# Diagonal-block inversions moved from GpSimd to VectorE, and a range check moved from VectorE to GpSimd, in a DeltaNet + PReLU kernel

## Chip, cores, metric

One core of one Trainium2 chip. The metric is the device time of one execution in microseconds (us), as the median of the runs of one kernel. All runs quoted here were in the fast state. The aim is to predict, from the profile of the kernel before alone, what the change does to the time, and then to find out by experiments which part of it did what.

## The reference

```python
def _attn_ref(q, k, v, beta):            # B=4, H=8, S=768, D=48
    k_n = k / (np.linalg.norm(k, axis=-1, keepdims=True) + 1e-06)
    state = np.zeros((B, H, D, D), dtype=np.float32)
    for t in range(S):
        kt, vt, bt = (k_n[:, :, t], v[:, :, t], beta[:, :, t, None])
        y[:, :, t] = np.einsum('bhd,bhde->bhe', q[:, :, t], state)
        v_old = np.einsum('bhde,bhd->bhe', state, kt)
        state = state + bt[:, :, :, None] * np.einsum('bhd,bhe->bhde', kt, vt - v_old)

def _moe_ref(x, w_in, w_out, alpha):     # x: 3072 x 384 (from y), w_in: 384 x 2048, w_out: 2048 x 384
    h = x @ w_in
    g = np.maximum(h, 0.0) + alpha * np.minimum(h, 0.0)
    return g @ w_out
```

The weights `w_in` and `w_out` arrive as float64 and are converted to fp32 on the chip.

## The kernel before

The attention runs in 24 steps (12 chunks of 64 tokens, two pairs of batches). Each step needs the inverse of triangular 64 x 64 matrices, which is built from inverses of their 32 x 32 diagonal blocks. These are computed by elimination in seven batches: the first on VectorE, the other six on GpSimd. In parallel the weights are converted in 56 pieces (24 of `w_in` with 256 columns, 32 of `w_out` with 192), each of which passes ScalarE (two instructions), VectorE (two), GpSimd (an add) and VectorE again (the range check, which sets numbers too small for fp32 to zero). `weave` mixes the instruction streams, and each engine runs its own in order.

Names used below: `inv` is the inverse of a step's matrix, built from the diagonal blocks (`diag`), the masked key products `kk` and an intermediate `mid`; `r` is the step's right-hand side, `u` its scaled product with `inv`, and `a_t` the masked products of queries and keys. The FFN is the part with `w_in` and `w_out`, and `g` is its hidden layer after the activation. "u of step 0 reaches TensorE" is the start of the first matmul that reads it.

```python
# one piece of the weights' conversion; temp(...) has two buffers
last = temp("last")
nc.scalar.activation(last, lo, ACT.Copy, scale=2.0**-29)
size = temp("size").bitcast(FP32)
nc.scalar.square(size, hi.bitcast(FP32))
high = dst.bitcast(U32)
nc.vector.tensor_scalar(out=high, in0=hi, ...)              # L179
nc.vector.scalar_tensor_tensor(out=high, in0=hi, ...)       # L183
nc.gpsimd.tensor_tensor(out=high, in0=high, in1=last, op=ALU.add)          # L187
nc.vector.scalar_tensor_tensor(out=dst, in0=size, scalar=LEAST * LEAST, in1=dst,
                               op0=ALU.is_ge, op1=ALU.mult)                # L188
# ... (cut)
def eliminate(m, eng):                   # batch m; HB = 32
    r = block[m][0:np_]
    for j in range(1, HB - 1):
        # ... prod = 0:np_ partitions x j*(31-j)
        eng.tensor_tensor(out=prod, in0=..., in1=..., op=ALU.mult)                    # L362
        eng.tensor_tensor(out=r[:, 0:j, j + 1 : HB], in0=r[:, 0:j, j + 1 : HB],
                          in1=prod, op=ALU.add)                                       # L368
        yield
    nc.gpsimd.memset(r.rearrange("p r c -> p (r c)")[:, :: HB + 1], 1.0)              # L372
    flipped = work.tile([128, HB, HB], FP32, name="flipped", bufs=1)
    eng.tensor_copy(out=flipped[0:np_], in_=r.rearrange("p r c -> p c r"))            # L374
    # ... (two DMAs to DRAM, from which each step fetches its blocks)
# ... (cut)
FIRST = [b[0] for b in batches]          # batch 1 is woven into step 0, batch 2 into step 4, ...
for n in range(N):
    gens = [(attention(n), 4)]
    if n + 2 in FIRST:
        gens.append((eliminate(place[n + 2][0], nc.gpsimd), HB - 1))
    # ... 5 pieces of w_in in each of steps 0 to 3; from step 4 on FFN and w_out
    weave(*gens)
```

## Time and profile before

| | before |
|---|---|
| time, median of 3 runs | 887.39 us (887.05 to 888.3) |
| TensorE busy | 748.6 us |
| u of step 0 reaches TensorE (L472) | 97.6 us |
| conversion of `w_out`, first VectorE instruction to last check | 176.3 to 260.5 us |
| first matmul of the FFN's second product (L530) | 259.2 us |

The profile's first page of the kernel before: span, busy time of each engine (PE is TensorE, PEld its weight loads, DVE VectorE, ACT ScalarE, POOL GpSimd), and for three engines the busy share in 40 equal slices of 22.1 us, in tenths.

```profile
span 885.7 us, 20961 instructions
PE 748.6 (85%) x8917; PEld 574.9 (65%) x8917; DVE 289.2 (33%) x731; ACT 181.2 (20%) x402; POOL 281.6 (32%) x507
PE   4310678813779999999999999999999999999998
DVE  4870545514761313323233132131221312213030
POOL 5158522387330005811007700028447300000000
```

From the 13th slice on TensorE is full. What is to be gained lies in the slices before, where its digits fall to 0 and 1 while GpSimd (POOL) shows 8.

### The profile page before, as it was taken

Reading aid. Unit: us, or ns where it says so; the run is one execution under the profiler, and the core shown is the slowest. Engines: PE = TensorE matmul, PEld = TensorE weight load, DVE = VectorE, ACT = ScalarE, POOL = GpSimd, SP = SyncE. Lnnn points to the kernel's source line nnn. Section 1 sums busy time; section 2 is a strip of 40 time slices with the busy share of each in tenths; the row PEclk is TensorE's granted clock in tenths of the full one; section 3 lists DMA queues with packets and bytes.
Section 4 is the critical chain, followed back from the end, with each engine's and each line's share of the span. In section 5 each row is a group of like instructions: output and inputs, shape, how many; then the busy total and the mean of one; then the engine's idle time right before and its main releaser. Section 6 shows DMA issues by size and latency. Waiting matters only on the chain.

```text
span 885.7 us, 20961 instructions
## 1 busy us (share of the span) xinstructions
PE 748.6 (85%) x8917; PEld 574.9 (65%) x8917; DVE 289.2 (33%) x731; ACT 181.2 (20%) x402; POOL 281.6 (32%) x507
## 2 busy tenths in 40 slices
PE   4310678813779999999999999999999999999998
PEld 3210667712556868768778687786877868778684
DVE  4870545514761313323233132131221312213030
ACT  2210233312341202213112121120211212112020
POOL 5158522387330005811007700028447300000000
PEclk9999978555789999999999999999999999999999
DMA  5771166621353323062221252311422311000000
GB/s 102 158 158 42 26 174 159 143 78 47 99 144 63 61 42 64 23 117 58 56 56 33 57 111 39 69 38 28 105 48 42 73 31 22 1 20 2 10 10 18
DMA packets 183549, 58.10 MB, mean 66 GB/s; under 512 B 168592, under 2 KB 175776, under 8 KB 183456
## 3 DMA queue, kind: packets, MB, share of 16 engines
q1 hardware_dynamic: 183008, 56.66, 29.1%
q8 instruction: 70, 1.15, 0.5%
q10 hardware_dynamic: 448, 0.11, 0.1%
q14 instruction: 23, 0.19, 0.1%
HBM read 39.43 MB, written 17.30 MB: 64 GB/s over the span
## 4 chain that ended last, share of the span: by engine, by line
PE 77%; POOL 8%; DVE 7%; issue 3%; DMA 3%; SPq 1%; ACT 1%; POOLq 0%; ACTq 0%; DVEq 0%
PE p_ffn L530 28%; PE p_ffn L510 28%; POOL block L368 4%; POOL prod L362 3%; PE p_one L472 3%; PE p_one L415 3%; PE p_big L443 3%; PE p_one L458 3%; PE p_big L303 2%; PE p_one L404 2%; PE p_big L276 2%; PE p_one L499 1%; PE p_big L478 1%; DVE prod L362 1%; DVE block L368 1%
## 5 line engine op out<-in xcount | busy, mean ns | idle before, releaser
L510 PE MATMUL p_ffn<-xt,w_in 128*128 128x256 f32 x1152 | 274.4, 394 | 22.2 <-DVE g L521 19.8
L510 PEld LDWEIGHTS p_ffn<-xt,w_in 128*128 128x128 f32 x1152 | 222.1, 197 | 57.2 <-DVE g L521 14.1
L530 PE MATMUL p_ffn<-w_out,g 128*128 128x384 f32 x768 | 257.6, 489 | 0.0
L530 PEld LDWEIGHTS p_ffn<-w_out,g 128*128 128x128 f32 x768 | 143.1, 190 | 91.4
L521 DVE SCALAR_TENSOR_TENSOR g<-low,al_t,p_ffn 128x256 f32<-128x256 f32 x192 | 84.0, 477 | 178.9 <-ACT low L518 178.9
L362 POOL TENSOR_TENSOR prod<-block 128x30 f32<-128x30 f32 (+19 forms) x180 | 87.5, 486 | 41.1 <-DMA block<-image 22.9
L368 POOL TENSOR_TENSOR block<-block,prod 128x30 f32<-128x30 f32 (+19 forms) x180 | 92.9, 516 | 13.3
L518 ACT ACTIVATE low<-p_ffn 128x512 f32<-128x512 f32 x96 | 57.3, 596 | 167.9 <-PE p_ffn L510 159.1
L428 POOL TENSOR_TENSOR v_raw<-v_raw,norm 128x384 f32<-128x384 f32 x24 | 19.9, 830 | 211.0 <-DMA v_raw<-in_v_dram 204.2
L266 POOL TENSOR_TENSOR mask<-minus,wgt 128x512 f32<-128x512 f32 x24 | 25.2, 1049 | 104.5 <-DVE kk L309 86.4
L404 PE MATMUL p_one<-diag,kk 64*64 64x32 f32 x768 | 30.6, 231 | 25.3 <-POOL prod L362 21.5
L458 PE MATMUL p_one<-r,inv 64*64 64x48 f32 x768 | 31.6, 239 | 23.8 <-POOL prod L362 23.8
L415 PE MATMUL p_one<-diag,mid 64*64 64x32 f32 x768 | 30.9, 235 | 23.4 <-ACT mid L407 22.8
L458 PEld LDWEIGHTS p_one<-r,inv 64*64 64x64 f32 x768 | 28.5, 154 | 33.4 <-POOL block L368 23.9
L415 PEld LDWEIGHTS p_one<-diag,mid 64*64 64x64 f32 x768 | 28.3, 152 | 31.4 <-ACT mid L407 23.3
L404 PEld LDWEIGHTS p_one<-diag,kk 64*64 64x64 f32 x768 | 28.5, 149 | 27.1 <-POOL prod L362 21.6
L472 PEld LDWEIGHTS p_one<-u,a_t 64*64 64x64 f32 x768 | 27.4, 149 | 20.4 <-DVE u L460 9.4
L472 PE MATMUL p_one<-u,a_t 64*64 64x48 f32 x768 | 30.5, 234 | 11.6 <-DVE u L460 11.6
L174 ACT ACTIVATE last<-words 128x192 uint32<-128x192 uint32 (+1 forms) x56 | 22.5, 401 | 87.0 <-POOL w_in L187 45.0
L537 ACT COPY o_sb<-p_ffn 128x384 f32<-128x384 f32 x24 | 11.5, 479 | 129.4 <-PE p_ffn L530 129.4
L446 DVE TENSOR_TENSOR r<-v_raw,p_big 128x384 f32<-128x384 f32 x22 | 12.2, 553 | 69.9 <-PE p_big L443 68.6
L486 DVE TENSOR_TENSOR y<-y,p_one 128x384 f32<-128x384 f32 x22 | 12.2, 554 | 59.6 <-PE p_one L472 59.6
(75 smaller groups left out, 619.4 us busy)
## 6 DMA issues: line engine op xcount, KB each, us to landing
image<-kk SPq DMA_DIRECT2D x24, 256.0 KB
words<-in_moe_w_in_dram SPq DMA_DIRECT2D x24, 256.0 KB
words<-in_moe_w_out_dram SPq DMA_DIRECT2D x32, 192.0 KB
ke<-in_k_dram SPq DMA_DIRECT2D x48, 96.0 KB
qp<-in_q_dram SPq DMA_DIRECT2D x48, 96.0 KB
v_raw<-in_v_dram SPq DMA_DIRECT2D x48, 96.0 KB
kl<-in_k_dram SPq DMA_DIRECT2D x48, 96.0 KB
out_dram<-o_sb SPq DMA_DIRECT2D x48, 96.0 KB
```

What stands on the lines that cost most here:

```text
L266: nc.gpsimd.tensor_tensor(out=mask, in0=minus[:, None, :].to_broadcast([128, H, C]), in1=wgt.rearrange("p a g -> p (a g)")[:, :, None].to_ ...
L362: eng.tensor_tensor(out=prod, in0=r[:, 0:j, j : j + 1].to_broadcast([np_, j, n]), in1=r[:, j : j + 1, j + 1 : HB].to_broadcast([np_, j, n] ...
L368: eng.tensor_tensor(out=r[:, 0:j, j + 1 : HB], in0=r[:, 0:j, j + 1 : HB], in1=prod, op=ALU.add)
L404: nc.tensor.matmul(p[half(t), h], kk[n][half(t), h], diag[n % NE][half(t), h, 0:HB])
L415: nc.tensor.matmul(p[half(t), h], mid[n % 2][half(t), h], diag[n % NE][half(t), h, HB:C])
L443: nc.tensor.matmul(p[half(t), a, w, g], x[n][dims(a), g, half(t)], state[bp][dims(a), t, g])
L458: nc.tensor.matmul(p[half(t), h], inv[n % NE][half(t), h], rhs_[n][half(t), h])
L472: nc.tensor.matmul(p[half(t), a, g], a_t[n][half(t), a * G + g], us[n][half(t), a * G + g])
L510: nc.tensor.matmul(p_h[:, i], w_in[:, t, (f + i) * 128 : (f + i + 1) * 128], xt[:, t], start=(t == 0), stop=(t == KT - 1),)
L518: nc.scalar.activation(low, p_h, ACT.Relu, scale=-1.0)
L521: nc.vector.scalar_tensor_tensor(out=g[:, i], in0=low[:, i], scalar=al_t[:, f + i : f + i + 1], in1=p_h[:, i], op0=ALU.mult, op1=ALU.add,)
L530: nc.tensor.matmul(p_o, gs[f // 2][:, f % 2, bp * 128 : (bp + 1) * 128], w_out[:, f], start=(f == 0), stop=(f == FT - 1),)
```

## The change

The intent: take the inversions, which TensorE waits for, from the slower engine to the faster one (an elimination instruction of 128 x 238 elements takes 0.62 us on GpSimd in the kernel before and 0.40 on VectorE in the kernel after), and make room for them on VectorE by giving GpSimd the range check and small products.

```diff
             nc.scalar.square(size, hi.bitcast(FP32))
+            nc.gpsimd.tensor_scalar(
+                out=size, in0=size, scalar1=LEAST * LEAST, scalar2=None, op0=ALU.is_ge
+            )
@@
             nc.gpsimd.tensor_tensor(out=high, in0=high, in1=last, op=ALU.add)
-            nc.vector.scalar_tensor_tensor(
-                out=dst, in0=size, scalar=LEAST * LEAST, in1=dst,
-                op0=ALU.is_ge, op1=ALU.mult,
-            )
+            nc.gpsimd.tensor_tensor(out=dst, in0=dst, in1=size, op=ALU.mult)
@@ prep: two products of 128 x 8 per step
-        bt = beta_t[:, c, bp]
-        nc.vector.tensor_tensor(out=bt, in0=bt, in1=rec, op=ALU.mult)
-        nc.vector.tensor_tensor(
+        nc.gpsimd.tensor_tensor(out=beta_t[:, c, bp], in0=beta_t[:, c, bp], in1=rec, op=ALU.mult)
+        nc.gpsimd.tensor_tensor(
             out=wgt,
@@ through_state: no copy for the first chunk (the two steps with c == 0); solve() indexes accordingly
+        if c == 0:
+            rhs_[n] = by_parity(nv[n])
+            return
         r = work.tile([128, H, D], FP32, name="r")
-        if c == 0:
-            nc.gpsimd.tensor_copy(out=r.rearrange("p (a g) d -> p a g d", a=2), in_=by_parity(nv[n]))
-            rhs_[n] = r
-            return
@@ the loop over steps
         if n + 2 in FIRST:
-            gens.append((eliminate(place[n + 2][0], nc.gpsimd), HB - 1))
+            gens.append((eliminate(place[n + 2][0], nc.vector), HB - 1))
```

In the kernel after, the lines are L178 (compare), L190 (add), L191 (multiply), L361 and L367 (elimination), L458 (u), L470, L508 and L528 (matmuls that were L472, L510 and L530).

> **What bounds the kernel now.** I first cut the span into five stretches, with the busy time of each engine in each (after the engines: granted TensorE clock, DMA share, GB/s).
>
> ```profile
> 0.00:53.00 53.00, 19.00 (x273) 14.57 (x273) 35.77 (x109) 12.32 (x29) 17.32 (x40) 1.00 0.67 127
> 53.00:104.00 51.00, 12.49 (x264) 12.08 (x265) 14.56 (x41) 8.04 (x23) 37.95 (x70) 1.00 0.27 68
> 104.00:176.00 72.00, 58.04 (x1193) 51.18 (x1191) 40.98 (x104) 24.21 (x61) 21.07 (x29) 0.74 0.63 149
> 176.00:260.00 84.00, 38.46 (x377) 30.94 (x376) 44.96 (x123) 28.07 (x79) 52.78 (x94) 0.65 0.36 100
> 260.00:886.00 626.00, 620.58 (x6819) 466.16 (x6817) 152.97 (x357) 108.53 (x211) 152.45 (x276) 1.00 0.22 46
> ```
>
> From 260 us on TensorE is busy 620.6 of 626 us at full clock. That part is a fixed amount of matmul: it starts when the weights' conversion and attention steps 0 to 5 are done, and the end follows 626 us later. So the change gains only by an earlier start of that part, and loses wherever VectorE makes TensorE wait inside it. Before it TensorE is idle in two blocks, both while GpSimd (POOL) inverts a batch of diagonal blocks. The timelines of TensorE, VectorE and GpSimd there:
>
> ```profile
> 57.31 0.23 POOL L362 TENSOR_TENSOR prod<-block 128x30 f32<-128x30 f32 x1
> 86.85 0.71 DVE L188 SCALAR_TENSOR_TENSOR w_in<-size,w_in 128x256 f32<-128x256 f32 x1 [23.49 <-POOL w_in L187]
> 93.53 1.91 POOL L374 COPY flipped<-block 128x1024 f32<-128x1024 f32 x1
> 97.61 1.83 PE L472 MATMUL p_one<-u,a_t 64*64 64x48 f32 x29 [7.14 <-DVE u L460]
> ```
>
> The inversion runs on GpSimd from 57.3 to 95.4 us. One add of the weights' conversion (L187) stands behind most of it in GpSimd's order, VectorE's range check (L188) waits 23.5 us for that add, and u of step 0, behind the check, reaches TensorE at 97.6. The second block is the same from 174.9 to 213.6 us, with two such waits (17.7 and 10.2 us). The chain that ended last agrees: 77% of it is TensorE, 8% GpSimd, 7% VectorE.
>
> **What the skill says, and the trace.** "SBUF — State Buffer", section "Who interferes with whom": a VectorE instruction with two SBUF inputs, or in a two-port mode, and a GpSimd instruction that reads SBUF exclude each other; the later one blocks. The trace agrees, at a point where v_raw ran on GpSimd from 49.00 to 49.83 and a copy from 49.90 to 50.40:
>
> ```profile
> 48.88 0.24 DVE L362 TENSOR_TENSOR prod<-block 64x84 f32<-64x84 f32 x1
> 49.15 0.77 DVE L368 TENSOR_TENSOR block<-block,prod 64x84 f32<-64x84 f32 x1
> 49.96 0.51 DVE L362 TENSOR_TENSOR prod<-block 64x58 f32<-64x58 f32 x1
> 50.50 0.21 DVE L368 TENSOR_TENSOR block<-block,prod 64x58 f32<-64x58 f32 x1
> ```
>
> The same size takes 0.24 us free and 0.77 us blocked. Likewise L183 on 192 elements: 0.35 free, 0.75 blocked (medians of 14 each). Instructions reading PSUM (g at L521, u at L460) keep 0.47 and 0.55 us either way.
> "VectorE: DVE Perf Modes", section on the TRN2 errata, gives (N+151)/0.96 ns for an fp32 tensor_tensor: 407 ns at N = 240; the trace has 400. "GPSIMD Engine Reference", section 3.1, has 2.6 cycles per element for two inputs on GpSimd and about 1.8 for a tight loop; the trace's mask (512: 1.05 us) and v_raw (384: 0.83 us) give 0.17 us + 1.7 ns per element, less than 2.6 cycles at the page's 1.2 GHz (2.2 ns) would be.
>
> **Part by part.**
> *Inversion on VectorE.* A batch has 60 tensor_tensor on j(31-j) elements, 4960 summed over j, so 9920 in all. On VectorE (batch 0, rows by shape: 30 elements 0.19 us, 240 elements 0.40) one costs 0.16 us + 1 ns per element: 60 x 0.16 + 9.9 = 19.5, plus 60 gaps of 0.035 = 21.6 us, plus 1.0 for the flip. On GpSimd it took 38 us with what stood between. Six batches move: two (45 us) before the matmul-bound part, four (90 us) inside it.
> *Range check to GpSimd.* VectorE loses 56 instructions (32 of 0.34, 24 of 0.41: 21 us) and with them every wait for the add. GpSimd gets a compare and a multiply per piece. Estimates from its other rows: compare like a copy (384: 0.51 us) 0.40 us for 192 elements and 0.46 for 256; multiply by the fit above 0.50 and 0.61. With the add (0.60, 0.74) and three gaps of 0.08 a piece is 1.75 us (w_out) or 2.05 us (w_in), against 0.6 and 0.74 before. GpSimd becomes the pace of the conversion: 32 x 1.75 = 56 us for w_out.
> *Weights' small products (beta_t, wgt) to GpSimd and no copy of the right-hand side.* 48 small instructions of 0.2 us move to where there is room, two copies of 0.5 us go; none on the path. About 1 us.
>
> *Stretch 53 to 104.* I read the compiled instruction orders of the two kernels against each other: TensorE's is practically the same; on VectorE u of step 0 comes after 48 of the 60 inversion instructions and four conversion pieces. Inversion starts near 59.6 (a_t, three pieces, three norms ahead of it), 48 instructions are 18.2 us, the conversion between 3.2, blocking by GpSimd perhaps 2: u at 83 instead of 97, a gain of 14 us. The inverse goes out later in the DMA queue, behind kk of step 6, which shifts by the same 14.
> *Stretch 104 to 176.* Bursts of three to five conversion pieces now pass at 2.05 us on GpSimd instead of 1.3 to 1.7, and ScalarE's copies stand behind them (two buffers for its temporaries). One to two us in each of three steps: a loss of 3. Net 11 us earlier at the end of the stretch, r of step 5 near 165.
> *Stretch 176 to 260.* From r of step 5 to the end of the conversion it took 84 us. After: 13 inversion steps first (10 us), then GpSimd has 96 instructions of mean 0.50 us and 0.08 gap, and VectorE about 99 that exclude it. Each then blocks the other; the trace shows GpSimd's instructions little lengthened (0.59 to 0.64) and VectorE's doubled (0.35 to 0.75), so I take 0.58 + 0.10 per GpSimd instruction: 65 us, with mask, v_raw and the flip 70. Sum 80 to 81, a gain of 3 us. I chose this over full serialization (below). So the matmul-bound part starts 14 us earlier.
> *Inside the matmul-bound part.* An attention step is 31.5 us there (start to start of L443). VectorE's own work is 7.7 us of it (153/626); an inversion adds 22.6, and some blocking: over 30 us, so VectorE is full for that step. Walking the new VectorE order of step 8: inversion starts at 350.6, and g for the second-last L510 group is done near 370.8 instead of 365.9. TensorE starts L530 at 366.7 and its third p_ffn tile needs that buffer (two of them): about 4 us of waiting. In steps 12, 16 and 20 fewer g lie in the inversion, but inv and a_t come late: 1, 1 and 1 to 2 us. Sum 7 to 8.
> The sum: 887.4 - 14 + 7 = 880.
>
> **Rivals.** (1) *The lock makes the conversion as slow as before.* If in the stretch from 176 every VectorE and GpSimd instruction simply added up, it would be 10 + 96 x 0.86 = 93 us instead of 84, the 11 us gained earlier would shrink to 2, and with 7 lost later the time would be about 892; for it speaks that GpSimd and VectorE together are already busy 98 of 84 us there. Against it: their overheads overlap. (2) *VectorE becomes the bound in the steps with an inversion.* If TensorE waits 6 to 8 us in each of four, the loss is 24 to 32 us: about 900. For it: over 30 of 31.5 us; against: an inversion needs to be ready only for the step after next, and the static order leaves 4 to 7 us of FFN matmuls between each product and its use. (3) *The long waits vanish altogether.* TensorE idles 38 us from 53 to 104 and 45 us from 176 to 260; if the conversion flows freely beside the inversion on VectorE and the chain follows TensorE, 30 to 35 us are gained and nothing is lost later: about 855. For it: no instruction on the attention path now waits for GpSimd's in-order queue behind an inversion.
>
> **Range and chances.** Mid 880. The front may gain from 2 (rival 1) to 30 us (rival 3), the later part may lose 2 to 25 us; they are independent, so 8 in 10 is 860 to 898. Over 2% faster is below 869.6, over 2% slower above 905. Faster 0.25 (mostly rival 3), same 0.68, slower 0.07 (rival 2 together with rival 1).
>
> **What would show it.** Right: in the profile after, u of step 0 reaches L472 near 83 us; conversion's multiply on GpSimd ends near 246; GpSimd busy about 1.5 us per piece; VectorE busy about 289 - 21 - 9 + 6 x 20.5 (inversions without gaps) = 382 us, plus 20 or more of blocking; TensorE busy unbroken from about 246 us except for waits on g, r or a_t from VectorE in four steps, 7 us together. Wrong: inversion instructions on VectorE well over 0.6 us on average in the front (the lock rules: rival 1); waits of TensorE for g over 5 us in several later steps (rival 2); L530 of the first chunk starting before 235 us (rival 3). The estimate that carries most is GpSimd's compare and multiply: at 0.8 us each the conversion alone takes 76 us and the gain is gone.

## The result, and the profile after

| | before | after |
|---|---|---|
| time, median (range) of 4 runs each | 887.22 us (886.69 to 888.3) | 873.2 us (872.68 to 874.94) |
| ratio, 95% interval | | 0.9844 (0.9827 to 0.9861) |
| mean granted TensorE clock of the profiled run | 0.945 | 0.950 |

The ratio here and below is the mean time of one kernel's fast runs over that of the kernel before's fast runs of the same rounds, so it is not quite the ratio of the medians. The change gains 14 us or 1.6%: the interval of the ratio lies clear of 1. But it is within 2%, so it counts as "same". The output is correct.

The first page of the kernel after, the same rows, with the chain that ended last:

```profile
span 870.9 us, 20922 instructions
PE 745.9 (86%) x8917; PEld 571.9 (66%) x8917; DVE 389.9 (45%) x993; ACT 182.9 (21%) x402; POOL 185.1 (21%) x299
PE   4311886463499999999999999999999999999998
DVE  3789736786513227724037632248439403213030
POOL 6242758588740010001001001000000000000000
PE 71%; POOL 2%; DVE 1%; issue 0%; ACT 0%; ACTq 0%; POOLq 0%
```

GpSimd's hump at the fourth slice, the inversion, is gone. TensorE's hole there is only a little shorter: 1 1 8 in the third to fifth slices, against 1 0 6 before. And GpSimd now shows 8 5 8 8 7 4 in the 7th to 12th slices, where TensorE has 6 4 6 3 4 9. The shares of the chain sum to 74%: the view followed it back only to about 220 us, so they cannot be set beside the shares that the prediction quotes.

TensorE's timeline of the kernel after, the lines with the large waits before the matmul-bound part and the first L528 (start, duration, and in brackets the idle time and what ended it):

```profile
82.97 1.94 PE L456 MATMUL p_one<-v_raw,inv 64*64 64x48 f32 x32 [18.56 <-issue]
85.77 1.83 PE L470 MATMUL p_one<-u,a_t 64*64 64x48 f32 x29 [0.85 <-DVE u L458]
216.76 1.11 PE L441 MATMUL p_big<-state,k_t 48*64 48x48 f32 x32 [9.70 <-DVE a_t L317]
237.40 4.89 PE L508 MATMUL p_ffn<-xt,w_in 128*128 128x256 f32 x12 [10.52 <-POOL w_out L191]
242.13 3.07 PE L528 MATMUL p_ffn<-w_out,g 128*128 128x384 f32 x9
```

u of step 0 arrives at 85.8 instead of 97.6, and the first matmul of the second product at 242.1 instead of 259.2: 17.0 us earlier. From that matmul to the end it takes 628.8 us (870.9 - 242.13), against 626.6 before, a loss of 2.2. Together that is the 14.8 us by which the profiled spans differ.

The stretches of the kernel after (busy us of PE, PEld, DVE, ACT, POOL; granted clock; DMA share; GB/s). The cuts are those before the prediction's last three stretches, each 14 us earlier, so they meet the same events only roughly:

```profile
90.00:162.00 72.00, 56.81 (x1272) 49.73 (x1271) 40.50 (x93) 27.94 (x70) 51.24 (x70) 0.83 0.64 147
162.00:246.00 84.00, 41.43 (x382) 33.34 (x378) 55.97 (x144) 26.76 (x75) 63.45 (x97) 0.63 0.37 102
246.00:871.00 625.00, 618.32 (x6810) 464.31 (x6808) 229.22 (x582) 109.22 (x213) 32.33 (x54) 1.00 0.22 46
```

The middle row is the one to look at: GpSimd is busy 63 of 84 us, against 53 before, although the inversion has left it. Between the same events, from r of step 5 to the last `w_out` piece, it took 89.3 us (159.9 to 249.3), against 84.7 before. Its groups between 150 and 265 us, and a stretch of its timeline:

```profile
L178 POOL TENSOR_SCALAR size<-size 128x192 f32<-128x192 f32 (+1 forms) x35 | 25.0, 715 | 8.5 <-ACT size L177 5.7
L190 POOL TENSOR_TENSOR w_out<-w_out,last 128x192 uint32<-128x192 uint32 x32 | 22.2, 697 | 11.0 <-DVE w_out L186 9.2
L191 POOL TENSOR_TENSOR w_out<-w_out,size 128x192 f32<-128x192 f32 x32 | 19.8, 619 | 2.1
```
```profile
207.95 0.69 POOL L178 TENSOR_SCALAR size<-size 128x192 f32<-128x192 f32 x1
208.72 0.59 POOL L190 TENSOR_TENSOR w_out<-w_out,last 128x192 uint32<-128x192 uint32 x1
209.38 0.59 POOL L191 TENSOR_TENSOR w_out<-w_out,size 128x192 f32<-128x192 f32 x1
210.06 0.69 POOL L178 TENSOR_SCALAR size<-size 128x192 f32<-128x192 f32 x1
```

Here GpSimd goes from piece to piece at 2.1 us each (210.06 - 207.95), with gaps of 0.1 us or less. From its first add to its last multiply of `w_out` (170.0 to 249.3) it has only three pauses over 0.3 us, 7.1 us together. How this reaches TensorE is seen by following the wait of 10.52 us back through ScalarE and VectorE, again from the timelines of the kernel after:

```profile
233.88 0.37 ACT L177 ACTIVATE size<-words 128x192 f32<-128x192 f32 x1 [1.62 <-POOL w_out L191]
234.16 0.58 ACT L516 ACTIVATE low<-p_ffn 128x512 f32<-128x512 f32 x1
234.63 0.51 ACT L249 ACTIVATE ksq<-ke 128x384 f32<-128x384 f32 x1
235.18 0.55 DVE L251 TENSOR_REDUCE norm<-ksq 128x8 f32<-128x384 f32 x1 [9.08 <-ACT ksq L249]
236.44 0.82 DVE L519 SCALAR_TENSOR_TENSOR g<-low,al_t,p_ffn 128x256 f32<-128x256 f32 x2
```

ScalarE's `size` waits for a multiply on GpSimd, because `size` has two buffers. `low` and `ksq` stand behind it in ScalarE's order; VectorE, idle for 9 us, waits for `ksq`; g stands behind the norm in VectorE's order; and g frees the PSUM buffer that L508 needs. The view puts the wait of L508 down to L191, which ended at 237.28; the two g ended at 237.26. A matmul of `xt` and `w_in` needs no `w_out`, so I read g as the cause. Either way the wait leads back to GpSimd's order.

### The profile page after: what moved, and what is told of

It reads as the page before. It is cut to its first block, busy times and chain, and to the rows that moved or that the text cites. A ratio compares the mean times of both kernels' runs of the same rounds, so it can differ in the third digit from the quotient of the medians.

```text
span 870.9 us, 20922 instructions
## 1 busy us (share of the span) xinstructions
PE 745.9 (86%) x8917; PEld 571.9 (66%) x8917; DVE 389.9 (45%) x993; ACT 182.9 (21%) x402; POOL 185.1 (21%) x299
## 4 chain that ended last, share of the span: by engine, by line
PE 71%; POOL 2%; DVE 1%; issue 0%; ACT 0%; ACTq 0%; POOLq 0%
PE p_ffn L528 29%; PE p_ffn L508 27%; PE p_one L456 2%; PE p_one L414 2%; PE p_big L441 2%; PE p_one L470 2%; PE p_one L403 2%; PE p_big L302 2%; PE p_big L275 1%; PE p_one L497 1%; PE p_big L476 1%; POOL size L178 1%; POOL w_out L191 1%; POOL w_out L190 1%; DVE block L367 0%
## 5 line engine op out<-in xcount | busy, mean ns | idle before, releaser
L508 PE MATMUL p_ffn<-xt,w_in 128*128 128x256 f32 x1152 | 272.0, 391 | 16.2 <-POOL w_out L191 10.5
L528 PE MATMUL p_ffn<-w_out,g 128*128 128x384 f32 x768 | 257.7, 489 | 1.6 <-DVE g L519 1.6
L508 PEld LDWEIGHTS p_ffn<-xt,w_in 128*128 128x128 f32 x1152 | 220.1, 195 | 50.9 <-POOL w_out L191 10.7
L528 PEld LDWEIGHTS p_ffn<-w_out,g 128*128 128x128 f32 x768 | 143.0, 190 | 93.3 <-ACT low L516 1.9
L361 DVE TENSOR_TENSOR prod<-block 128x84 f32<-128x84 f32 (+22 forms) x210 | 74.4, 354 | 9.4 <-DMA ke<-in_k_dram 3.9
L367 DVE TENSOR_TENSOR block<-block,prod 128x84 f32<-128x84 f32 (+22 forms) x210 | 75.7, 360 | 6.0
L178 POOL TENSOR_SCALAR size<-size 128x192 f32<-128x192 f32 (+1 forms) x56 | 44.0, 786 | 14.5 <-ACT size L177 10.2
L257 POOL TENSOR_TENSOR beta_t<-beta_t,rec 128x8 f32<-128x8 f32 x24 | 5.2, 218 | 184.1 <-DVE rec L255 184.1
L414 PE MATMUL p_one<-diag,mid 64*64 64x32 f32 x768 | 30.1, 232 | 15.1 <-ACT mid L406 14.6
L414 PEld LDWEIGHTS p_one<-diag,mid 64*64 64x64 f32 x768 | 27.5, 149 | 23.2 <-ACT mid L406 15.1
L470 PEld LDWEIGHTS p_one<-u,a_t 64*64 64x64 f32 x768 | 28.2, 152 | 14.1 <-issue 6.9
L470 PE MATMUL p_one<-u,a_t 64*64 64x48 f32 x768 | 31.2, 238 | 5.2 <-DVE u L458 5.2
L458 DVE TENSOR_TENSOR u<-p_one,wgt 128x384 f32<-128x384 f32 x24 | 13.3, 556 | 46.9 <-PE p_one L456 46.9
```

The costliest lines, as they stand in the source:

```text
L178: nc.gpsimd.tensor_scalar(out=size, in0=size, scalar1=LEAST * LEAST, scalar2=None, op0=ALU.is_ge)
L361: eng.tensor_tensor(out=prod, in0=r[:, 0:j, j : j + 1].to_broadcast([np_, j, n]), in1=r[:, j : j + 1, j + 1 : HB].to_broadcast([np_, j, n] ...
L414: nc.tensor.matmul(p[half(t), h], mid[n % 2][half(t), h], diag[n % NE][half(t), h, HB:C])
L470: nc.tensor.matmul(p[half(t), a, g], a_t[n][half(t), a * G + g], us[n][half(t), a * G + g])
L508: nc.tensor.matmul(p_h[:, i], w_in[:, t, (f + i) * 128 : (f + i + 1) * 128], xt[:, t], start=(t == 0), stop=(t == KT - 1),)
L528: nc.tensor.matmul(p_o, gs[f // 2][:, f % 2, bp * 128 : (bp + 1) * 128], w_out[:, f], start=(f == 0), stop=(f == FT - 1),)
```

## Experiments

Eleven kernels ran. The theory after the result: moving the inversion alone gains about twice as much, and GpSimd's range check gives half of it back. Rivals: the later four batches on VectorE cost time in the matmul-bound part; the lock between VectorE and GpSimd stretches the inversion; the wait for the diagonal's memset, which stayed on GpSimd, is what holds VectorE.

| run | time, median (range), us | ratio, 95% interval |
|---|---|---|
| e1 only the inversion moved | 860.08 (858.19 to 863.68) | 0.9696 (0.9660 to 0.9731) |
| e2 all but the inversion | 903.37 (901.57 to 904.2) | 1.0170 (1.0146 to 1.0193) |
| e3 change, later four batches on GpSimd | 874.79 (874.3 to 875.38) | 0.9851 (0.9831 to 0.9871) |
| e4 change, diagonal's memset on VectorE | 869.44 (868.13 to 871.42) | 0.9792 (0.9769 to 0.9816) |
| e5 change, no range check | 852.36 (849.03 to 855.67) | 0.9622 (0.9585 to 0.9658) |
| e6 change, check on VectorE | 859.61 (858.75 to 861.88) | 0.9708 (0.9681 to 0.9734) |
| e7 change, no compare (wrong result) | 858.88 (855.93 to 860.85) | 0.9693 (0.9662 to 0.9723) |
| e8 change, check of `w_out` on VectorE | 861.51 (858.59 to 863.22) | 0.9714 (0.9679 to 0.9749) |
| e9 before, inversion and memset on VectorE | 862.26 (857.01 to 864.14) | 0.9705 (0.9681 to 0.9729) |
| e10 change, check and memset on VectorE | 860.85 (853.38 to 862.29) | 0.9674 (0.9642 to 0.9705) |
| e11 before, only batch 1 on VectorE | 874.41 (871.65 to 876.14) | 0.9847 (0.9826 to 0.9869) |

e1 to e4, e5 to e8 and e9 to e11 each ran on one chip together. The kernel before took 887.83, 885.95 and 887.42 us there; the change itself was timed with 887.22, so a difference between runs of different groups is uncertain by a further 1 to 2 us. In the profiled executions of all thirteen kernels the part from the first matmul of the FFN's second product to the end takes 626.0 to 629.3 us. So nearly all that separates them arises before it.

### e1: the inversion alone

Edit, to the kernel before:
```diff
-            gens.append((eliminate(place[n + 2][0], nc.gpsimd), HB - 1))
+            gens.append((eliminate(place[n + 2][0], nc.vector), HB - 1))
```


> The kernel before with only the inversion of all batches on VectorE. Theory A (the gain is the inversion leaving GpSimd's in-order queue; the range check on GpSimd costs more than it saves, since GpSimd's compare took 0.69 us per w_out piece and the conversion then passes at 2.0 us a piece): 862 to 872 us, at or below the changed kernel's 873. Rival B (the range check's move is what ends VectorE's waits, and VectorE with inversion and check is overloaded from 160 to 250 us): 878 us or more.

Measured: 860.1 us, just below the range of theory A. One line of the change gains twice what the whole change gains. TensorE's timeline of e1, and GpSimd's add between 150 and 265 us:

```profile
223.07 5.46 PE L510 MATMUL p_ffn<-xt,w_in 128*128 128x256 f32 x12 [3.85 <-DVE g L521]
228.32 1.25 PE L530 MATMUL p_ffn<-w_out,g 128*128 128x384 f32 x2
```
```profile
L187 POOL TENSOR_TENSOR w_out<-w_out,last 128x192 uint32<-128x192 uint32 x32 | 20.4, 642 | 38.6 <-DVE w_out L183 30.3 <-ACT size L177 6.6 <-ACT last L174 1.8
```

Here GpSimd waits for VectorE (30.3 us), not the other way round, the conversion ends at 229.7 instead of 249.3, and L530 starts at 228.3, 13.8 us before the changed kernel's. u of step 0 arrives at 85.6, as in the changed kernel (85.8): once the inversion is on VectorE, the check makes no difference at the front.

### e2: everything but the inversion

Edit, to the kernel after: batches 1 to 6 back on GpSimd.
```diff
-            gens.append((eliminate(place[n + 2][0], nc.vector), HB - 1))
+            gens.append((eliminate(place[n + 2][0], nc.gpsimd), HB - 1))
```


> The changed kernel with its later batches inverted on GpSimd again, all else as changed. Theory A: GpSimd has the inversions and two more instructions a piece in one order, the first long block stays and the w_out stretch grows by about 32 x 1.3 = 40 us less what was idle: 895 to 925 us. Rival B: VectorE no longer waits for GpSimd's add, so at least half of the 14 us stays: 880 or below.

Measured: 903.4 us, so the rest of the change is a loss of 16 us by itself. Two of the long waits of TensorE in e2:

```profile
106.87 0.42 PE L414 MATMUL p_one<-diag,mid 64*64 64x32 f32 x3 [31.73 <-ACT mid L406]
229.01 5.22 PE L508 MATMUL p_ffn<-xt,w_in 128*128 128x256 f32 x12 [16.77 <-POOL w_out L191]
```

With check and inversion both on GpSimd, ScalarE is held behind GpSimd, and TensorE waits for ScalarE's `mid` for 31.7 us, and again for 20.6 us at 200.8. Rival B was not all wrong: u of step 0 reaches TensorE at 70.2 us, 27 us earlier than in the kernel before, as VectorE no longer waits for GpSimd's add. But r of step 5 comes at 178.6, against 175.8 before: the gain is lost again in the wait for `mid`.

### e3: the later four batches back on GpSimd

Edit, to the kernel after:
```diff
-            gens.append((eliminate(place[n + 2][0], nc.vector), HB - 1))
+            gens.append((eliminate(place[n + 2][0], nc.vector if n < 8 else nc.gpsimd), HB - 1))
```


> The changed kernel with batches 1 and 2 inverted on VectorE, batches 3 to 6 (steps 8, 12, 16, 20) on GpSimd as before. If the inversions inside the matmul-bound part cost TensorE only the 1.6 us wait for g near 351 us and a few short ones (the saturated part took 633.5 us after against 631.5 before, from its first L510 to the end): 871 us, 2 us faster than the changed kernel. If they cost the 7 us that the prediction put there: 866. If the later batches on VectorE are free: 873.

Measured: 874.8 us against 873.2, above all three expected values: no difference that the intervals of the ratios show, and no gain. From the first matmul of the second product to the end e3 takes 627.8 us and the change 628.8. So the later four inversions, for which VectorE is busy 76 us more in the matmul-bound part (229.2 - 153.0), cost about 1 us there, if anything. Rival 2 of the prediction falls.

### e4: the diagonal's memset on VectorE

Edit, to the kernel after:
```diff
-        nc.gpsimd.memset(r.rearrange("p r c -> p (r c)")[:, :: HB + 1], 1.0)
+        eng.memset(r.rearrange("p r c -> p (r c)")[:, :: HB + 1], 1.0)
```


> The changed kernel with the memset of the diagonal on VectorE too. In the changed kernel this one memset stands on GpSimd behind conversion pieces, and VectorE's flip waits 6.9 us for it at 207 to 214 us, which TensorE sees as a 9.7 us wait before L441. Theory C (that wait is on the path): 865 to 870. Rival D (GpSimd's conversion at 2.0 us per piece sets the end of the stretch whatever VectorE does): within 1 us of 873.

Measured: 869.4 us, 4 us better than the change (the intervals of the ratios do not meet). First VectorE's timeline of the changed kernel, then TensorE's of e4:

```profile
214.32 1.03 DVE L373 COPY flipped<-block 128x1024 f32<-128x1024 f32 x1 [6.91 <-POOL block L371]
```
```profile
211.40 1.10 PE L441 MATMUL p_big<-state,k_t 48*64 48x48 f32 x32 [3.11 <-DVE a_t L317]
```

In the changed kernel VectorE's flip waits 6.9 us for a memset of 0.15 us that stands behind conversion pieces in GpSimd's order, and a_t stands behind the flip. With the memset on VectorE the wait of L441 is 3.1 instead of 9.7 us. Part of that is lost again: the next L508 then waits 11.1 us, as GpSimd's pace is unchanged.

### e5, e6, e7: how many GpSimd instructions a piece has

Edits, to the kernel after: e5 drops the compare and the multiply; e6 puts VectorE's check back; e7 drops only the compare, so the weights are multiplied by `size` and the result is wrong on purpose (relative error 2.13).

```diff
# e5
-            nc.gpsimd.tensor_scalar(
-                out=size, in0=size, scalar1=LEAST * LEAST, scalar2=None, op0=ALU.is_ge
-            )
-            nc.gpsimd.tensor_tensor(out=dst, in0=dst, in1=size, op=ALU.mult)
# e6
-            (the same four lines)
+            nc.vector.scalar_tensor_tensor(
+                out=dst, in0=size, scalar=LEAST * LEAST, in1=dst, op0=ALU.is_ge, op1=ALU.mult)
# e7
-            nc.gpsimd.tensor_scalar(
-                out=size, in0=size, scalar1=LEAST * LEAST, scalar2=None, op0=ALU.is_ge
-            )
```


> The changed kernel without any range check (weights below the limit come out wrong on purpose): one GpSimd instruction a piece, as before the change, and no check on VectorE. Theory A (GpSimd's instructions per piece set the pace of the w_out stretch, 2.0 us a piece in the changed kernel): GpSimd is no longer the pace, VectorE has 32 checks fewer than in the run with only the inversion moved (860): 852 to 860 us. Rival E (the inversion on VectorE sets the w_out stretch, GpSimd only fills in): 868 to 873.

> The changed kernel with only the range check back on VectorE; the small products on GpSimd and the unused copy stay as changed. If those two are off the path, as predicted (about 1 us): 858 to 861, the same as the run with only the inversion moved. If GpSimd's small products in the way of the mask cost something: 862 or more.

> The changed kernel without the compare, multiplying by the size itself (wrong on purpose): two GpSimd instructions a piece. Theory A: a w_out piece takes 1.28 us of work and 0.16 of gaps, 1.45 instead of 2.05, so 32 pieces take up to 19 us less, of which the run with only the inversion moved shows 13 to be usable; between: 860 to 866 us, nearer to one instruction a piece than to three because VectorE's 1.1 us a piece with the inversion then takes over. If the loss of the range check's move were a lock effect on VectorE in proportion to GpSimd's busy time: in the middle, 866 to 868.

Measured: with three GpSimd instructions per piece (the change) 873.2, with two (e7) 858.9, with one (e5) 852.4 us, none of them with a check on VectorE. e6, with one on GpSimd and the check on VectorE, takes 859.6. I had called e5 wrong on purpose; its result is correct, as this input's weights hold no number that the check would catch. It is a kernel for measuring, not for use.

GpSimd's groups between 150 and 265 us in e7:

```profile
L187 POOL TENSOR_TENSOR w_out<-w_out,last 128x192 uint32<-128x192 uint32 x32 | 22.1, 690 | 19.1 <-DVE w_out L183 15.8 <-ACT last L174 3.1
L188 POOL TENSOR_TENSOR w_out<-w_out,size 128x192 f32<-128x192 f32 x32 | 20.2, 631 | 2.5
```

With two instructions GpSimd waits 15.8 us for VectorE (9.2 in the changed kernel) and ends its `w_out` pieces at 232.2 instead of 249.3. Its pauses over 0.3 us between the first and the last of these come to 13.1 of 59.4 us, against 7.1 of 79.2. So it is the third instruction that turns GpSimd into the pace: 13 to 14 us come with it (e7 lies just below its expected range, 860 to 866), and another 6 with the second (e7 against e5; the intervals do not meet). Whether the number of instructions matters, or only their time (0.7 us for the compare), these runs do not separate; more buffers for `size` and `last` were not tried. The check on VectorE costs about 7 us by itself (e6 against e5; the intervals do not meet). And e6 differs from e1 only in the small products and the copy: 859.6 and 860.1 us, and ratios of 0.9708 and 0.9696, so these parts are worth nothing that can be measured.

A kernel with the check as one `scalar_tensor_tensor` on GpSimd, which would have had two instructions and a right result, does not compile (error NCC_IBIR766, "cannot run on engine Pool"); there is no run of it.

### e8: the check of w_in on GpSimd, that of w_out on VectorE

Edit, to the kernel after (the multiply is split in the same way; `else` is VectorE's check as in e6):
```diff
+            if w is w_in:
                 nc.gpsimd.tensor_scalar(
                     out=size, in0=size, scalar1=LEAST * LEAST, scalar2=None, op0=ALU.is_ge
                 )
```


> The changed kernel with the check of w_in on GpSimd and that of w_out on VectorE. Theory A puts the whole loss of the range check's move in the w_out stretch (160 to 250 us): 859 to 862 us. If the check of w_in on GpSimd costs its part too (24 of 56 pieces): about 866.

Measured: 861.5 us, like e6 (859.6; the intervals overlap). So the loss lies in the `w_out` stretch, where 32 pieces follow each other; no cost of the check of `w_in` stands clear of the scatter. In the `w_in` stretch five pieces go with each step, so I take it that GpSimd has the time.

### e9, e10: looking for the best version

Edits: e9 is e1 and e10 is e6, each with the memset of e4.

> The kernel before with the inversion and its diagonal memset on VectorE, nothing else. In the run with only the inversion moved the flip no longer stood long behind GpSimd, so the memset should matter little: 858 to 860 us. If GpSimd's order still holds it: 856 or less.

> The changed kernel with the range check back on VectorE and the diagonal memset on VectorE: 857 to 860 us, the best version without giving up the check; a difference from the run before it in this job of more than 1.5 us would be the small products and the copy.

Measured: 862.3 and 860.9 us, both above what I had expected, but like e1 and e6 within the scatter (the six runs of e10 spread over 9 us). The memset shows a cost only in e4, where GpSimd's queue is full of conversion pieces. e1, e6, e9 and e10 cannot be told apart by these runs. All four are correct and about 3% faster than the kernel before; e1 is the smallest edit.

### e11: only the first batch that GpSimd had

Edit, to the kernel before:
```diff
-            gens.append((eliminate(place[n + 2][0], nc.gpsimd), HB - 1))
+            gens.append((eliminate(place[n + 2][0], nc.vector if n == 0 else nc.gpsimd), HB - 1))
```


> The kernel before with only batch 1 inverted on VectorE (step 0), the rest on GpSimd. The prediction put 14 us on the first long wait; the changed kernel has u of step 0 at 85 us against 97 and r of step 5 at 160 against 176. If all of that comes from batch 1: 887 less 12 to 16, 871 to 875 us, and batch 2 brings the other 12 to 15 of the run with only the inversion moved. If batch 2 brings most: 880 or more.

Measured: 874.4 us: batch 1 alone is worth 13 us. From here to e1 (860.1) it is another 14. As batches 3 to 6 moved nothing in e3, I put these to batch 2, though e3 had the check on GpSimd and the same was not tried with it on VectorE. The profiles agree: the second product starts at 245.2 us in e11 and at 228.3 in e1, 17 us earlier, and the part from there on takes 626.0 and 628.7 us, so up to 3 us of it are given back by the later batches.

The account of the change is then: batch 1 -13, batch 2 and later -14, range check on GpSimd +13 (873.2 - 860.1), small products and copy 0: together -14.

## Why the prediction was right or wrong, point by point

The time was right (880 predicted, 873.2 measured, inside 860 to 898), and so was "same", the outcome given the highest chance. But the gain was put at 7 us and is 14, and two of its terms were wrong in sign. The steps:

- **What bounds the kernel: right.** From L528 on TensorE is busy 622.2 of 628.8 us, before 621.4 of 626.6. The gain came from an earlier start.
- **u of step 0 at 83, a gain of 14: right, a little large.** Measured 85.8 and a gain of 11.8. The wait before the matmuls with the inverse (L458, now L456) went from 23.8 to 18.6 us, and that for u from 7.1 to 0.85.
- **Stretch 104 to 176, a loss of 3: wrong in sign.** r of step 5 came at 159.9 instead of 175.8, so 4 us more were gained. One part had not been foreseen: from step 3 to step 4 (18.9 us between their L458 before, 15.1 between their L456 after) the granted clock was 0.50 before and 0.87 after, with TensorE busy 15.3 and 10.5 us for the same 299 matmuls. Why the clock was higher there is not settled by these runs, and it is not firmly the change's doing: e3, which has the change's instructions up to step 8, was granted 0.70 there and gained only 1.1 us in the stretch. So these single profiles do not show a loss of 3, but give the gain only as 1 to 4 us.
- **r of step 5 to the end of the conversion in 81 us, a gain of 3: wrong.** It took 89.3 against 84.7, a loss of 4.6. The mis-sized term is GpSimd's three instructions: estimated 0.40 (compare), 0.60 (add) and 0.50 (multiply), 1.5 us per `w_out` piece; measured 0.70, 0.69 and 0.62, so 2.0, or 32 x 0.5 = 16 us more in all, part of which lay beside other waits. The compare is the worst: I had put it at the cost of a copy. The multiply came from a fit through `mask` and `v_raw`, which read a broadcast operand; its median is 0.59 us, that of the add beside it. A wait was also missed: the memset that VectorE's flip needs stayed on GpSimd, behind the pieces (6.9 us; e4 shows it worth 4).
- **The start of the matmul-bound part 14 us earlier: nearly right** (17.0), **but by luck**: 2 us less at u of step 0, 7 more in the middle. The last term was a gain of 1.2 us (3 predicted) and not the loss of 4.6 only because the second product did not wait for the end of the conversion, as the prediction had it: it started 7 us before (242.1 and 249.3), and only 1.3 us before in the kernel before (259.2 and 260.5).
- **7 to 8 us lost in the matmul-bound part: too large.** 2.2 were lost. In it TensorE has one wait over 0.6 us, of 1.55 us for g at 351.4, which is the one placed at step 8 with 4 us. VectorE was busy 389.9 us in all, 8 more than the 382 worked out, where 20 or more were put on for blocking. In e3, without the four inversions on VectorE, the part is only 1 us shorter.
- **Small products and copy, about 1 us: not to be distinguished from nothing** (e6 against e1).
- **Rival 1 (the lock) is false.** Between 160 and 210 us batch 2's instructions on VectorE are busy 24.0 us in the changed kernel, and 19.8 in e1, where GpSimd has a third as many instructions per piece. That is 4 us, not a serial sum. And e7 took 858.9 us, where a lock in proportion to GpSimd's busy time would have given 866 to 868. In the front (55 to 92 us) they take 0.39 us on average, where the prediction had named "well over 0.6" as the sign of this rival. For the conversion its 93 us were nearer to the measured 89.3 than the prediction's 81, but for another reason, GpSimd's three instructions.
- **Rival 2 (VectorE the bound in the steps with an inversion) is false**, by e3 and the 1.55 us.
- **Rival 3 (the waits vanish, 855) was the nearest to what the inversion can do:** e1 reaches 860.1. What I did not see is that the change itself stands in its way. I had written that the estimate of compare and multiply carries most, but priced the check only for its own length, and not as what decides between 860 and 873. My warning that at 0.8 us each "the gain is gone" was too strong as well: at 0.70 and 0.62 the conversion took 80 us (from VectorE's first instruction for `w_out`, 169.1, to 249.3), and 14 us of gain were left, because it began earlier and the second product takes up the `w_out` pieces one after another.

## What to carry to other kernels

When a loop of small pieces passes several in-order engines, add up the instructions per piece on each: a third instruction of 0.7 us turned an engine with slack into the pace and held ScalarE, VectorE and TensorE behind it, by temporaries with two buffers and the order of instructions. A change made of several moves should be run move by move: here one line gained 27 us and the range check gave 13 back, and the sum looked like a small success. Price an operation from a row of its own kind, and when an instruction chain moves to another engine, look for the one small instruction in it (here a memset of 0.15 us) that stayed behind.

## What the Trainium skill lacked or had wrong

- "GPSIMD Engine Reference", section 3.1, gives cycles for a two-input instruction and a tight loop, but none for the built-in compare with a constant (`tensor_scalar`). Here it took 0.70 us for 192 elements and 0.90 us for 256 on average, longer than the two-input multiply on the same shapes (0.62 and 0.74 us).
- The same section's 2.6 cycles per element (2.2 ns at its 1.2 GHz) for two inputs fit the conversion's multiply, contrary to what the prediction's comparison suggests: medians of 0.59 us for 192 elements and 0.73 for 256, so about 2.1 ns per further element. The section has no figure for an operand that is repeated by broadcast. Here such instructions took less than that slope would give: 0.83 us for 384 elements (v_raw) and 1.05 for 512 (mask).
- "SBUF — State Buffer", section "Who interferes with whom", says that the later of the two engines fully blocks. The runs fit for VectorE (0.35 to 0.75 us in the kernel before). What the page does not give is how much this comes to over a stretch of mixed work. Here it was little: inversion instructions 24.0 us busy beside three GpSimd instructions per piece, 19.8 beside one.
- No page says that the compiler refuses a `scalar_tensor_tensor` on GpSimd. It does (error NCC_IBIR766, for the one-instruction check above).
